# Windowed attention with a two-layer MLP: cross-partition copies and low parts on GpSimd, normalising on ScalarE

## The chip, the cores and the metric

The kernel runs on one core of one Trainium2 chip. A core has TensorE (PE in the profile), VectorE (DVE), ScalarE (ACT), GpSimd (POOL) and SyncE (SP), which issues the DMAs. The metric is the device time of one execution in microseconds, lower is better; several runs give a median.

## What is computed

```python
# attention: 8 batches, 8 heads, 576 tokens, head size 64, float32
scores = q @ k.T / sqrt(64)
mask_plain = (rel >= 0) & (rel < 32)                       # heads 0 to 3
mask_dil   = (rel >= 0) & (rel < 128) & (rel % 4 == 0)     # heads 4 to 7
attn = softmax(where(mask, scores, -1e9)) @ v
# MLP: x is the attention's result as [4608, 512]
h = x @ w_in                                               # [512, 2048]
g = h * clip(h + 3, 0, 6) / 6
out = g @ w_out                                            # [2048, 512]
```

rel is the query's position less the key's.

## The kernel before

**Precision.** Float32 matmuls are done as three matmuls of a cheaper kind: each factor is split into a high part (a rounded copy) and a low part (what the copy left out), and high x high, high x low and low x high are added up in PSUM.

**Attention** is cut into 48 trios (a group of four heads and a third of a batch's rows, 12 query blocks of 32 rows each). The first 12 are done in an opening whose order is written out by hand. The other 36 are done in blocks on TensorE (`attend`): a block multiplies the scores of trio b and the values of trio b-2. For the scores DVE adds the mask (L264) and takes the row maxima (L290), POOL scales the maxima (L294), ACT takes the exponents (L302, six groups of 64 columns), DVE transposes 32 by 32 blocks (`turn_by_blocks`, L404 and L405), and ACT copies the parts that must change partitions (`cross`, L412, four copies of 32x192, tile `a`).

For the values the result must be divided by its row sums. There are two ways. A trio in `SHARED` (17 of the 36) has DVE make the reciprocals (`share`, L310, L311) and ACT multiply, six operations of 64 columns (`shares`, L321). The other 19 are normalised by DVE alone (`normalise`, L326, L327, L329). Either frees the PSUM bank. Then the result `x` goes the same way as the exponents: DVE transposes, and ACT copies across partitions (L412, tile `xf`). What follows (`high`, L477, and `low`, L483 and L485) splits it for the MLP or copies it into `raw`; `low` is on POOL here.

**The MLP** has two forms. The first 1536 tokens (four chunks of 384) are done plainly: `gemm1` (L571 to L573) into `ps_h`, ACT's `relu` (L579), DVE's `gate` (L582), the high part `gh` (L586, by ACT in the opening, by POOL afterwards), DVE's low part `gl` (L590), and `gemm2` (L621 to L623) two steps later. The other 3072 tokens, in three groups of 1024, use a scheme of seven products in place of eight: sums and differences of weight blocks are made once, split into high and low, written to DRAM (`sums` for the first layer, `rights` for the second) and streamed back through `ring` buffers. For each of 2 x 8 pairs of weight blocks `combine` has DVE add up the parts (L691) and make four sums (L699), ACT take the high part (L703, 128x1024), and DVE the low part (L708, 128x1024); then five DMAs of SP store them (`combo_out`, `combo_plain`). A group runs the first layer's products (L798 to L800), with copies and gates on ACT and DVE (L1111, L1118, L1071, L1076), and then the second layer's (L789), whose factors are split by ACT (L1252, `gh`) and DVE (L1256, `gl`).

**Order.** Behind the opening every operation is put into a plan with its engine, an estimated duration, what it waits for and which buffers it takes and frees. TensorE's order is given; `_in_time` works out a latest start for each operation and goes through the plan, taking on each engine what can start soonest, and among these the one that is due first. This fixes the order of ACT, DVE, SP and POOL, each of which works through its own in order.

Of the kernel before, what the change touches and what calls it, by code (L numbers as in the profile page):

```python
# [20 lines left out]
QB = 32  # L21
# [17 lines left out]
EVER = 1.0e6  # L39
# [5 lines left out]
LATER = 2  # L45
LANDING = 2.6
PE_MASKS = frozenset()
SHARED = frozenset((0, 1, 2, 3, 4, 7, 8, 9, 10, 11, 12, 13, 14, 15, 27, 28, 32))
POOL_LOWS = frozenset((10, 11))
BESIDE = {(0, 0): 1, (0, 1): 2, (0, 2): 1, (0, 3): 2, (0, 4): 1, (0, 5): 2, (0, 6): 1, (0, 7): 1, **{(1, k): 1 for k in range(7)}}  # L50
HIGH_BY = ("aaaaaaaa",) * 7
# [34 lines left out]
def windowed_attention_ffn(ctx: ExitStack, tc: tile.TileContext, qk, vp, w, mask, out, out_t):  # L86
# [23 lines left out]
    nc = tc.nc  # L110
# [11 lines left out]
    CH = TB * QB  # L122
# [94 lines left out]
    es, ats, xs, xfs = {}, {}, {}, {}  # L217
# [187 lines left out]
        nc.vector.transpose(out=dst.rearrange("p (u i y) -> p u i y", u=2, y=QB), in_=twice)  # L405
        return dst, mid

    def cross(dst, mid, i):

        for c in (2 * i, 2 * i + 1):  # L410
            u, to = c % 2, c ^ 1
            ins = nc.scalar.copy(  # L412
                dst[QB * to : QB * (to + 1), u * CH // 2 : (u + 1) * CH // 2], mid[QB * c : QB * (c + 1), : CH // 2]
            )
        return ins


# [288 lines left out]
    def combo_low(side, k, i, n, eng):  # L706
        v, hi = (x[:, i * 4 // n : (i + 1) * 4 // n] for x in combos[side, k])
        eng.tensor_tensor(out=v.bitcast(F32R), in0=v, in1=hi.bitcast(F32), op=ALU.subtract)  # L708
# [10 lines left out]
    def combo_out(side, k):  # L719
        v, hi = combos.pop((side, k))  # L720
        for part, x in enumerate((hi.bitcast(F32), v)):
            if side:
                to = rights.rearrange("(i k) p a x -> k p i a x", k=PAIRS)[k][:, 0:4, part]
            else:
                to = sums[row(k, S2) : row(k, S2) + 4].rearrange("n p a x -> p n a x")[:, :, part]
            nc.sync.dma_start(out=to, in_=x)
# [111 lines left out]
    def op(engine, us, do, after=(), lag=0.0, takes=(), gives=(), before=(), ahead=AHEAD):  # L838
        plan.append(Operation(engine, us, do, [x for x in after if x is not None], lag, [(*x, 0)[:3] for x in takes], list(gives), list(before), ahead))
        if engine == "PE":  # L840
            beats.append(len(plan) - 1)
        return len(plan) - 1

    def transfer(us, size, do, after=(), takes=(), gives=(), ahead=EVER):
        x = op("SP", us, do, after, takes=takes, ahead=ahead)
        return op("DMA", size * 1.3, lambda: None, [x], lag=LANDING, gives=gives, ahead=EVER)

    ONE, TWO, SLOT = [("work", 1)], [("work", 2)], [("w", 1)]
# [1 line left out]
    raw_seen, freed = set(), []  # L850
    released = {"ps_h": [], "ps_a": freed}

    def turn_over(t, src, into, name, after):
        two = []

        def do():
            two.extend(turn_by_blocks(src.pop(t), name))
            into[t] = two[0]

        x = op("DVE", 0.92, do, [after], takes=TWO, gives=ONE, ahead=EVER)  # L860
        return [
            op("ACT", 0.7, lambda i=i: cross(*two, i), [x], gives=ONE if i else (), ahead=EVER) for i in range(2)
        ]

    def attend(bs, pools, whole=False):

        scores = [NFIRST + b for b in bs if NFIRST + b < T]
        values = [NFIRST + b - 2 for b in bs if b >= 2]
        couples = [(NFIRST + b, NFIRST + b - 2) for b in bs]
        order = [t for x in couples for t in x if t in scores + values]  # L870
        bank, room = dict(zip(order, pools)), {}

        def do():
            for x in couples:
                block(*(t if t in bank else None for t in x), [bank.get(t) for t in x], whole)

        names = {x: "ps_h" if bank[x] is ps_h else "ps_a" for x in order}
        for x in names.values():
            room[x] = room.get(x, 0) + 1
        beat = op(  # L880
            "PE", 0.35 + 0.3 * sum(by_tensor(t) for t in scores) + 0.535 * len(order), do,
            [*(x for t in values for x in turned[t]), *(landed_k.get(t) for t in scores), *(landed_v.get(t) for t in values),
             *(freed.pop(0) for _ in range(room.get("ps_a", 0)) if freed), *released["ps_h"][-2:][: room.get("ps_h", 0)]],
            takes=list(room.items()), gives=[("work", len(values))],
        )
        for ts in scores:
            x = beat
            if not by_tensor(ts):
                x = op("DVE", 0.55, lambda ts=ts: add_mask(ts), [beat], takes=ONE, gives=[(names[ts], 1)], ahead=EVER)
                released[names[ts]].append(x)  # L890
            x = op("DVE", 0.55, lambda ts=ts: plain_largest(ts), [x], ahead=EVER)
            x = op("POOL", 0.3, lambda ts=ts: scaled(ts), [x], ahead=EVER)
            for i in range(3):
                holds = not i and by_tensor(ts)
                x = op(
                    "ACT", 0.54, lambda ts=ts, i=i: exponents(ts, i), [x], takes=ONE if holds else (),
                    gives=[(names[ts], 1)] if i == 2 and by_tensor(ts) else (), ahead=EVER,
                )
            if by_tensor(ts):
                released[names[ts]].append(x)  # L900
            turned[ts] = turn_over(ts, es, ats, "a", x)
            if ts + NLOAD < T:
                landed_k[ts + NLOAD] = transfer(0.4, 0.82, lambda ts=ts: load_qk(ts + NLOAD), [beat])
        for tv in values:
            if tv - NFIRST in SHARED:
                x = op("DVE", 0.35, lambda tv=tv: share(tv), [beat], ahead=EVER)
                for i in range(3):
                    x = op(
                        "ACT", 0.5, lambda tv=tv, i=i: shares(tv, i), [x], takes=() if i else ONE,
                        gives=[(names[tv], 1)] if i == 2 else (), ahead=EVER,  # L910
                    )
            else:
                x = op("DVE", 0.9, lambda tv=tv: normalise(tv), [beat], takes=ONE, gives=[(names[tv], 1)], ahead=EVER)
            released[names[tv]].append(x)
            x = turn_over(tv, xs, xfs, "xf", x)
            if tv + NLOAD < T:
                landed_v[tv + NLOAD] = transfer(0.4, 0.77, lambda tv=tv: load_v(tv + NLOAD), [beat])
            pieces = [(n, place_of(token)[0]) for _, n, _, _, token in spans(tv)]
            kind = trios[tv][1]
            if any(c >= PLAIN for n, c in pieces):  # L920
                x = [*x, ends_of[1], *(combined[1, k][0] for k in range(PAIRS) if combo_place(1, k) == 1)]
            touched = {c for n, c in pieces if c >= PLAIN and (c, kind) not in raw_seen}
            raw_seen.update((c, kind) for c in touched)
            places = {}
            for c in touched:
                place = ("x1", 1) if (c - PLAIN, kind) in IN_ROOM else ("w", 1, 1)
                places[place[0]] = (place[0], places.get(place[0], (0, 0))[1] + 1, *place[2:])
            plain = [n for n, c in pieces if c < PLAIN]
            if plain:
                x = [op("ACT", sum(0.15 + n / 500 for n in plain), lambda tv=tv: high(tv), x, ahead=EVER)]  # L930
            split[tv] = op(
                "POOL", sum(0.25 + n / 250 for n, _ in pieces), lambda tv=tv: low(tv, nc.gpsimd), x, takes=list(places.values()), gives=ONE, ahead=EVER
            )
# [25 lines left out]
    def combine(side, k):  # L959
        place = combo_place(side, k)  # L960
        slots = "w" if place == "w" else f"x{place}"
        x = op(
            "DVE", 0.69, lambda: combo_words(side, k, 0, nc.vector), takes=[(slots, 2, SPARE[side][k])] if place == "w" else [(slots, 1, 1)],
            ahead=LEAD_SUMS,
        )
        words[side, k] = x = op("DVE", 0.69, lambda: combo_words(side, k, 1, nc.vector), [x], ahead=EVER)
        for i in range(4):
            x = op("DVE", 0.42, lambda i=i: combo_sum(side, k, i, nc.vector), [x], ahead=EVER)
        x = op("ACT", 1.05, lambda: combo_high(side, k), [x], takes=() if place == "w" else [(slots, 1)], ahead=EVER)
        x = op("DVE", 1.25, lambda: combo_low(side, k, 0, 1, nc.vector), [x], ahead=EVER)  # L970
        combined[side, k] = [
            transfer(0.9, 2.0, lambda: combo_out(side, k), [x], gives=[(slots, 2)]),
            transfer(1.35, 1.5, lambda: combo_plain(side, k), [x]),
        ]

    def last_use(side, f, x):
# [353 lines left out]
    with tc.manual_schedule(  # L1330
# [3 lines left out]
        for name in ORDER.split():  # L1334
            name, _, behind = name.partition("@")
# [261 lines left out]
```

## Time and profile before

| | |
|---|---|
| time, median of 3 runs | 830.58 us (830.51 to 830.89) |
| the profiled execution | 830.1 us, span 828.3 us, clock 0.995 |
| PE busy | 812.6 us (98%) |
| DVE busy | 634.7 us (77%) |
| ACT busy | 563.4 us (68%) |
| POOL busy | 128.5 us (16%) |
| ACT, copies of `xf` and of `a` (L412) | 50.4 and 50.4 us, 144 each of 350 ns |
| DVE, low parts of the sums (L708) | 20.7 us, 16 of 1294 ns |

The span is the time from the first to the last instruction of the profiled execution; busy time is the union of an engine's instructions. A line such as L412 is a line of the kernel. In a row of a group, the count is followed by the busy time in us, the mean of one in ns, the idle time of the engine just before these instructions, and what ended that idle time. In a row of the order of time stand the start, the duration (of several merged instructions together) and the instruction, with the idle time before it in brackets.

### The profile page before, as it was taken

What the parts mean: (1) busy time and instruction counts of PE and PEld (TensorE: products, weight loads), DVE (VectorE), ACT (ScalarE), POOL (GpSimd) and SP (SyncE); (2) the same over time, 40 slices, a digit from 0 to 9 for tenths busy, and PEclk for the clock granted to TensorE, in tenths of its full rate; (3) what the DMA queues carried; (4) which work ended last, traced back from release to release, by engine and by line L of the source; (5) the groups of instructions that cost most, each with busy time, mean ns of one, the idle gap of its engine ahead of it and who ended that gap; (6) DMA issues with size and microseconds to landing.
All of it is one profiled execution on the core that took longest, in us unless ns stands there. A gap on an engine that the chain in (4) does not pass through costs nothing.

```text
span 828.3 us, 20418 instructions
## 1 busy us (share of the span) xinstructions
PE 812.6 (98%) x8076; PEld 684.5 (83%) x8076; DVE 634.7 (77%) x1131; ACT 563.4 (68%) x1277; POOL 128.5 (16%) x192
## 2 busy tenths in 40 slices
PE   7999999999999999999999999999999999999998
PEld 4788999888889889888778888888888888888886
DVE  4989996568889898989869996665798834459943
ACT  3788776357997896879998564787656525446542
POOL 1338432112231224100121000010000000000000
PEclk9999999999999999999999999999999999999999
DMA  8757433257964989899885736867539379454632
GB/s 290 254 205 229 128 103 108 95 170 243 350 215 147 299 299 348 264 366 394 322 263 185 270 147 208 285 224 247 211 121 349 109 235 340 161 174 158 218 138 77
DMA packets 99455, 185.23 MB, mean 224 GB/s; under 512 B 6560, under 2 KB 35232, under 8 KB 99360
## 3 DMA queue, kind: packets, MB, share of 16 engines
q1 hardware_dynamic: 99360, 183.93, 64.9%
q8 instruction: 64, 1.05, 0.5%
q14 instruction: 31, 0.25, 0.1%
HBM read 145.10 MB, written 38.80 MB: 222 GB/s over the span
## 4 chain that ended last, share of the span: by engine, by line
PE 91%; ACT 5%; DMA 1%; DVE 1%; issue 1%; SPq 0%; DVEq 0%; ACTq 0%
PE ps_o L789 27%; PE ps_x L798 8%; PE ps_x L799 8%; PE ps_x L800 8%; PE ps_o L622 5%; PE ps_o L623 5%; PE ps_o L621 5%; PE ps_h L571 5%; PE ps_h L573 5%; PE ps_h L572 5%; PE ps_a L256 2%; PE ps_a L238 2%; DMA first<-in_v 1%; PE ps_b L256 1%; PE ps_b L238 1%
## 5 line engine op out<-in xcount | busy, mean ns | idle before, releaser
L789 PE MATMUL ps_o<-gh,ring 128*128 128x512 f32 x672 | 209.5, 389 | 0.7 <-ACT gh L1252 0.7
L789 PEld LDWEIGHTS ps_o<-gh,ring 128*128 128x128 f32 x672 | 126.1, 188 | 27.7 <-ACT gh L1252 1.5
L798 PE MATMUL ps_x<-cell,ring 128*128 128x512 f32 x336 | 132.5, 394 | 0.0
L789 PE MATMUL ps_o<-gl,ring 128*128 128x512 f32 x336 | 130.9, 390 | 0.6 <-DVE gl L1256 0.6
L799 PE MATMUL ps_x<-cell,ring 128*128 128x512 f32 x336 | 131.0, 390 | 0.0
L800 PE MATMUL ps_x<-cell,ring 128*128 128x512 f32 x336 | 130.8, 389 | 0.0
L1252 ACT CAST gh<-g 128x512 fp32r<-128x512 f32 x168 | 98.5, 620 | 46.1 <-PE ps_o L789 43.4
L1256 DVE TENSOR_TENSOR gl<-g,gh 128x512 fp32r<-128x512 f32 x168 | 109.5, 686 | 19.9 <-ACT gh L1252 9.1
L571 PE MATMUL ps_h<-x,wi 128*128 128x384 f32 x256 | 88.0, 344 | 0.2 <-DVE t L582 0.2
L573 PE MATMUL ps_h<-x,wi 128*128 128x384 f32 x256 | 86.2, 337 | 0.0
L572 PE MATMUL ps_h<-x,wi 128*128 128x384 f32 x256 | 85.9, 335 | 0.0
L623 PE MATMUL ps_o<-wo,gl 128*128 128x512 f32 x192 | 75.8, 395 | 0.0
L622 PE MATMUL ps_o<-wo,gh 128*128 128x512 f32 x192 | 75.6, 394 | 0.0
L621 PE MATMUL ps_o<-wo,gh 128*128 128x512 f32 x192 | 74.8, 389 | 0.3 <-PE ps_a L374 0.3
L789 PEld LDWEIGHTS ps_o<-gl,ring 128*128 128x128 f32 x336 | 63.1, 188 | 14.1 <-DVE gl L1256 1.2
L798 PEld LDWEIGHTS ps_x<-cell,ring 128*128 128x128 f32 x336 | 63.1, 188 | 13.8
L800 PEld LDWEIGHTS ps_x<-cell,ring 128*128 128x128 f32 x336 | 63.1, 188 | 13.3
L799 PEld LDWEIGHTS ps_x<-cell,ring 128*128 128x128 f32 x336 | 63.1, 188 | 12.9 <-DVE cell L773 0.4
L520 POOL TENSOR_SCALAR va<-st 128x512 f32<-128x512 f32 x32 | 53.9, 1688 | 75.0 <-DMA st<-in_w 67.0
L579 ACT ACTIVATE t<-ps_h,three 128x384 f32<-128x384 f32 x64 | 37.2, 583 | 40.4 <-PE ps_h L573 36.6
L302 ACT ACTIVATE e<-e,mx 128x64 f32<-128x64 f32 x216 | 56.6, 345 | 4.7 <-POOL mx L294 4.5
L1221 DVE TENSOR_TENSOR g<-g 128x1024 f32<-128x1024 f32 x48 | 57.4, 1217 | 0.0
(103 smaller groups left out, 1503.8 us busy)
## 6 DMA issues: line engine op xcount, KB each, us to landing
ring<-sums SPq DMA_DIRECT2D x84, 512.0 KB, 7.6
ring<-rights SPq DMA_DIRECT2D x84, 512.0 KB, 6.5
st<-in_w SPq DMA_DIRECT2D x32, 512.0 KB, 4.0
kq<-in_qk SPq DMA_DIRECT2D x39, 416.0 KB, 4.7
v<-in_v SPq DMA_DIRECT2D x39, 390.0 KB, 5.4
sums<-wi SPq DMA_DIRECT2D x24, 256.0 KB, 5.2
rights<-wo SPq DMA_DIRECT2D x24, 256.0 KB, 7.7
out<-o SPq DMA_DIRECT2D x11, 512.0 KB, 3.4
```

What stands on the lines that cost most here:

```text
L571: nc.tensor.matmul(ph, lhsT=wt(f, 0)[:, ks], rhs=a, start=(kt == 0), stop=False)
L572: nc.tensor.matmul(ph, lhsT=wt(f, 0)[:, ks], rhs=b, start=False, stop=False)
L573: ins = nc.tensor.matmul(ph, lhsT=wt(f, 1)[:, ks], rhs=a, start=False, stop=(kt == NK - 1))
L621: nc.tensor.matmul(po[c][tt], lhsT=gh[:, rows], rhs=wt(f, 2), start=first, stop=False)
L622: nc.tensor.matmul(po[c][tt], lhsT=gh[:, rows], rhs=wt(f, 3), start=False, stop=False)
L623: return nc.tensor.matmul(po[c][tt], lhsT=gl[:, rows], rhs=wt(f, 2), start=False, stop=(f == NF - 1))
L789: nc.tensor.matmul(banks[part], lhsT=right[:, a, cols], rhs=x, start=(start and not i), stop=(i == 2), skip_group_check=True)
L798: nc.tensor.matmul(bank, lhsT=tile_[:, 0, ks], rhs=h[:, kt], start=(start and kt == 0), stop=False, skip_group_check=True)
L799: nc.tensor.matmul(bank, lhsT=tile_[:, 0, ks], rhs=l[:, kt], start=False, stop=False, skip_group_check=True)
L800: nc.tensor.matmul(bank, lhsT=tile_[:, 1, ks], rhs=h[:, kt], start=False, stop=(kt == 1), skip_group_check=True)
L1252: nc.scalar.copy(two[0], gated_tile(g, q, k))
L1256: nc.vector.tensor_tensor(out=two[1], in0=gated_tile(g, q, k), in1=two[0].bitcast(F32), op=ALU.subtract)
```

## The change

Three things change. The four copies of each result across partitions (`xf`) go from ACT to POOL; those of the exponents (`a`) stay on ACT. All 36 later results are normalised by `share` and `shares`, that is by ACT with DVE's reciprocals; before it was 17. And the low part of the block sums is made by POOL in two halves of 128x512, where DVE made it in one operation; the stores wait for both halves. The durations given to the planner for these operations change with them.

```diff
-SHARED = frozenset((0, 1, 2, 3, 4, 7, 8, 9, 10, 11, 12, 13, 14, 15, 27, 28, 32))
+SHARED = frozenset(range(36))
...
-    def cross(dst, mid, i):
+    def cross(dst, mid, i, copy):
         for c in (2 * i, 2 * i + 1):
             u, to = c % 2, c ^ 1
-            ins = nc.scalar.copy(
-                dst[QB * to : QB * (to + 1), u * CH // 2 : (u + 1) * CH // 2], mid[QB * c : QB * (c + 1), : CH // 2]
-            )
+            ins = copy(dst[QB * to : QB * (to + 1), u * CH // 2 : (u + 1) * CH // 2], mid[QB * c : QB * (c + 1), : CH // 2])
         return ins
...
-    def turn_over(t, src, into, name, after):
+    def turn_over(t, src, into, name, after, by_pool=False):
...
         return [
-            op("ACT", 0.7, lambda i=i: cross(*two, i), [x], gives=ONE if i else (), ahead=EVER) for i in range(2)
+            op(
+                *(("POOL", 1.0) if by_pool else ("ACT", 0.7)),
+                lambda i=i: cross(*two, i, nc.gpsimd.tensor_copy if by_pool else nc.scalar.copy),
+                [x], gives=ONE if i else (), ahead=EVER,
+            )
+            for i in range(2)
         ]
...
-            x = turn_over(tv, xs, xfs, "xf", x)
+            x = turn_over(tv, xs, xfs, "xf", x, True)
...
-        x = op("DVE", 1.25, lambda: combo_low(side, k, 0, 1, nc.vector), [x], ahead=EVER)
+        lows_ = [op("POOL", 1.45, lambda i=i: combo_low(side, k, i, 2, nc.gpsimd), [x], ahead=EVER) for i in range(2)]
         combined[side, k] = [
-            transfer(0.9, 2.0, lambda: combo_out(side, k), [x], gives=[(slots, 2)]),
-            transfer(1.35, 1.5, lambda: combo_plain(side, k), [x]),
+            transfer(0.9, 2.0, lambda: combo_out(side, k), lows_, gives=[(slots, 2)]),
+            transfer(1.35, 1.5, lambda: combo_plain(side, k), lows_),
         ]
```

## The prediction

> **What bounds the kernel now.** I read the page first (busy time, waits), then the stages by window, then the order of single instructions where TensorE lost time.
>
> ```profile
> span 828.3 us, 20418 instructions
> PE 812.6 (98%) x8076; PEld 684.5 (83%) x8076; DVE 634.7 (77%) x1131; ACT 563.4 (68%) x1277; POOL 128.5 (16%) x192
> ```
>
> ```profile
> 160.00:336.00 176.00, 175.13 (x2585) 156.25 (x2585) 147.05 (x318) 140.68 (x420) 48.12 (x94) 1.00 0.77 253
> 336.00:371.00 35.00, 35.00 (x519) 28.22 (x518) 32.17 (x64) 27.19 (x62) 4.02 (x5) 1.00 0.91 307
> 371.00:433.00 62.00, 60.37 (x901) 48.14 (x899) 49.02 (x106) 59.56 (x152) 10.26 (x32) 1.00 0.92 327
> ```
>
> The window rows give the stretch, its length, then busy time of PE, PEld, DVE, ACT, POOL, the clock, DMA. TensorE is busy 98% and the clock is full (1.00). So the ceiling of any gain is what PE still loses, and the change touches only 160 to 583 us: before it runs the opening, written out by hand, after it no attention is left. Inside that, one stretch stands out: in 371 to 433 us ACT is busy 59.56 of 62.00 us (96%) and PE loses 1.6 us by the busy count. There ACT sets the pace. The rows give start, duration, and in brackets the idle time and what ended it:
>
> ```profile
> 429.20 0.39 PE L799 MATMUL ps_x<-cell,ring 128*128 128x512 f32 x1
> 429.42 0.39 PE L800 MATMUL ps_x<-cell,ring 128*128 128x512 f32 x1
> 430.14 0.50 PE L789 MATMUL ps_o<-gh,ring 128*128 128x512 f32 x1 [0.33 <-ACT gh L1252]
> 430.94 0.50 PE L789 MATMUL ps_o<-gl,ring 128*128 128x512 f32 x1 [0.30 <-DVE gl L1256]
> ...
> 431.97 0.40 PE L789 MATMUL ps_o<-gh,ring 128*128 128x512 f32 x1
> 432.72 0.50 PE L789 MATMUL ps_o<-gh,ring 128*128 128x512 f32 x1 [0.35 <-ACT gh L1252]
> 433.52 0.50 PE L789 MATMUL ps_o<-gl,ring 128*128 128x512 f32 x1 [0.29 <-DVE gl L1256]
> ```
>
> ACT in the same stretch, start and duration first:
>
> ```profile
> 428.00 1.44 ACT L412 COPY xf<-xf_t 32x192 f32<-32x192 f32 x4
> 429.46 0.62 ACT L1252 CAST gh<-g 128x512 fp32r<-128x512 f32 x1
> 429.99 0.58 ACT L1111 COPY s<-ps_x 128x512 f32<-128x512 f32 x1
> 430.59 1.44 ACT L412 COPY xf<-xf_t 32x192 f32<-32x192 f32 x4
> 432.05 1.14 ACT L1252 CAST gh<-g 128x512 fp32r<-128x512 f32 x2
> ```
>
> Matmul starts go every 0.22 us (429.20, 429.42). The four late ones start 0.72, 0.80, 0.75 and 0.80 us after the one before: 3.07 - 4 x 0.22 = 2.2 us lost. On ACT, four copies of a result across partitions (1.44 us) stand right ahead of each `gh` for which PE waits. These are the copies that the change takes off ACT.
>
> A second loss lies at 278 us, where the values of a block wait for copies of `a` (which stay on ACT):
>
> ```profile
> 277.65 0.24 PE L238 MATMUL ps_b<-kq 64*32 64x64 f32 x2
> 278.33 0.24 PE L256 MATMUL ps_a<-v,a 64*32 64x65 f32 x1 [0.38 <-ACT a L412]
> 279.06 0.24 PE L256 MATMUL ps_a<-v,a 64*32 64x65 f32 x1 [0.43 <-ACT a L412]
> ```
>
> 0.68 us passes between the first two starts, where such matmuls otherwise follow in hundredths; with the second wait of the same kind that is some 1.3 us.
>
> **The change part by part.**
>
> ```profile
> L412 ACT COPY xf<-xf_t 32x192 f32<-32x192 f32 x144 | 50.4, 350 | 2.3
> L321 ACT ACTIVATE x<-ps_a,z 128x64 f32<-128x64 f32 x84 | 19.3, 317 | 0.2
> L329 DVE TENSOR_TENSOR x<-ps_a,z 128x384 f32<-128x384 f32 x19 | 10.6, 558 | 0.9
> L708 DVE TENSOR_TENSOR v<-v,sh 128x1024 fp32r<-128x1024 f32 x16 | 20.7, 1294 | 0.4 <-ACT sh L703 0.2
> L485 POOL COPY raw<-xf 128x64 f32<-128x64 f32 x7 | 2.1, 300 | 9.3 <-ACT xf L412 8.4 <-DVE mx L290 1.0
> L485 POOL COPY raw<-xf 128x192 f32<-128x192 f32 x5 | 2.7, 531 | 16.1 <-DVE z L327 10.1 <-ACT xf L412 6.0
> L483 POOL TENSOR_TENSOR x<-xf,x 128x384 fp32r<-128x384 f32 x4 | 4.5, 1121 | 15.7 <-ACT x L477 15.7
> L483 POOL TENSOR_TENSOR x<-xf,x 128x192 fp32r<-128x192 f32 x3 | 2.1, 714 | 2.9 <-ACT x L477 2.9
> L520 POOL TENSOR_SCALAR va<-st 128x512 f32<-128x512 f32 x32 | 53.9, 1688 | 75.0 <-DMA st<-in_w 67.0 <-ACT wi L549 4.4 <-DVE va L539 1.4
> ```
>
> *Copies of the results.* 36 results x 4 copies leave ACT: 144 x 0.350 = 50.4 us. They go to POOL at a price the trace does not hold. Bounds: 0.300 us (64 columns) and 0.531 us (192 columns cut into strided pieces, on 128 partitions); a plain run of 192 lies between, I take 0.45. POOL +65 us, 1.8 us for a result instead of 1.4. What follows a copy is the copy into `raw` (L485), already on POOL and ahead of its need by far, so the longer latency costs nothing.
>
> *Normalising.* 19 results more go from DVE to ACT: DVE -19 x 0.558 = -10.6 us; the two small DVE operations on z stay; ACT +19 x 6 x 0.317 = +36.1 us. ACT in sum: -50.4 + 36.1 = -14.3 us, but by stage this differs. In 160 to 336 us four of the 19 (numbers 5, 6, 16, 17) add 4 x 1.90 = 7.6 us, and the copies of some 17 results go (17 x 1.40 = 23.8 us). In 336 to 371 four (18 to 21) add 7.6 us to 27.19 of 35 us, and no copies go there. In 371 to 433 five (22 to 26) add 9.5 us and these copies go:
>
> ```profile
> L412 ACT COPY xf<-xf_t 32x192 f32<-32x192 f32 x44 | 15.4, 350 | 0.7
> ```
>
> 59.56 - 15.4 + 9.5 = 53.7 us of 62. Over both stretches ACT ends at 88.4 of 97 us, two more than before, but the load moves to where ACT still had 7.8 us free. ACT then has 8 us of air in the stretch that ends in the 2.2 us loss, so I take all of that as gone.
>
> *Low parts of block sums.* 16 operations leave DVE (-20.7 us); 32 halves of 128x512 come to POOL. From 714 ns at 192 and 1121 ns at 384 columns the slope is 2.12 ns a column, 1.39 us at 512; bounds 1.12 and 1.69 us (a one-input POOL operation of that size). POOL +44 us, 2.8 us a sum instead of 1.29. Its five DMAs now wait for both halves, some 1.5 us later, and SP works in order, so ring loads and loads of keys and values queue behind. SP waits there already, longer than that:
>
> ```profile
> SPq L726 <- DVE v L708: 22.2, 9, 6.3
> ```
>
> Nine waits of the stores for L708, up to 6.3 us, reached no matmul by the waits of PE. So nothing for this; with that cover gone it would be the 1.5 us once or twice. POOL in sum: 128.5 + 65 + 44 = 238 us, 29% of the span; inside 160 to 433 us from 62 to some 155 of 273 us. Behind its new work queue the scaled maxima of the softmax (a block ahead of their use) and the 36 gates:
>
> ```profile
> 317.65 0.56 DVE L590 TENSOR_TENSOR gl<-t,gh 128x384 fp32r<-128x384 f32 x1 [0.60 <-POOL gh L586]
> 321.47 0.39 PE L621 MATMUL ps_o<-wo,gh 128*128 128x512 f32 x1
> ```
>
> This gate is the tightest of the 36: `gl` ends at 318.21 and PE takes it at 321.47, 3.3 us later. One half (1.39) or two copies (0.9) or both fit into that. Two halves and two copies, 3.7 us, do not: 0.4 us, which I count once.
>
> *Waits at 278 us.* ACT loses copies of results in 160 to 336 us and DVE 1.3 us for each sum, which gives the chain softmax, transpose, copies of `a` air; but the whole order behind the opening is planned anew from estimated durations. I take half of 1.3 us.
>
> **Sum.** -2.2 - 0.65 + 0.4 = -2.45 us. The profiled execution took 830.1 us, 1.8 us around its span of 828.3; the median of the runs is 830.58. So 827.65 for such an execution, 828.1 us as a median. About 0.2% (1.7 us) is what a measurement of this kernel tells from no change; the forecast is 0.3%.
>
> **The rivals.**
>
> *Nothing is gained.* The planner fills the freed ACT time with other work that stands ahead of `gh` in the same way (results 22 to 26 put six operations each there), and the wait at 278 us hangs on DVE's order. PE is at its pace elsewhere, so the time stays: 830.3 us.
>
> *POOL holds up the gates (the other side).* POOL works in order: a copy waiting for its DVE transpose, or a half waiting for the high part from ACT, holds every gate behind it. For it: the 16 sums run from 165.0 to 380.6 us and the gates (row below) from 163.7 to 337.0, so that 13 sums lie among them. Against: 3.3 us of cover at least. It decides where a hold exceeds 3.3 us. With halves at the 1.69 us bound, two halves and two copies make 4.4 us, 1.1 us a time; at a third of the 13 sums +4.8, less the 2.2: 833.2 us.
>
> *Banks held by ACT (the other side too).* A result normalised by DVE left its PSUM bank within some 0.9 us; by ACT it waits in a queue that is 90% full:
>
> ```profile
> 410.71 0.15 DVE L310 TENSOR_SCALAR z<-ps_b 128x6 f32<-128x6 f32 x1
> 415.13 0.52 ACT L321 ACTIVATE x<-ps_b,z 128x64 f32<-128x64 f32 x2
> ```
>
> Here from 410.71 to 415.65, 4.9 us, and no matmul waited, since the next block comes 42 matmuls of 0.22 us, 9.2 us, later. It decides when ACT falls more than 5 us further behind in 336 to 371 us (34.8 of 35 us by my count): 1 us at each of five blocks, +5 - 2.2: 833.4 us.
>
> *DVE and POOL block one another.*
>
> ```profile
> L590 DVE TENSOR_TENSOR gl<-t,gh x64: 517/553/1059, 42.0 to 338.4; 128x384 fp32r<-128x384 f32 x64
> L708 DVE TENSOR_TENSOR v<-v,sh x16: 1181/1218/1526, 165.0 to 380.6; 128x1024 fp32r<-128x1024 f32 x16
> L485 POOL COPY raw<-xf x73: 237/407/2928, 234.0 to 579.4; 128x96 f32<-128x96 f32 x16, 128x384 f32<-128x384 f32 x12, 128x128 f32<-128x128 f32 x11, 128x160 f32<-128x160 f32 x7
> L586 POOL CAST gh<-t x36: 498/567/1552, 163.7 to 337.0; 128x384 fp32r<-128x384 f32 x36
> ```
>
> Same shapes (minimum/median/maximum ns) take up to twice or thrice their median, on both engines, which looks like waiting for each other. A gate's chain could thus gain 0.5 (L590) + 1.0 (L586) behind one half and two copies (2.3): 3.8 us, 0.5 beyond the cover. At six such gates +3 us: 831.1. The Trainium skill, page "SBUF — State Buffer", section "SBUF: two separate sides", says that a DVE operation with two SBUF inputs and a GpSimd operation take the shared pair of ports by an exclusive lock, one blocking the other for a whole instruction. The spread of L590 and L586 agrees. By that rule alone all new POOL time under such DVE operations would come back as DVE time, and the 31 us taken off DVE would be no relief; the sum above does not use that relief save at 278 us.
>
> *More is gained.* All of 2.2 and 1.3 us and a little at other small waits before 433 us: 826.5 us.
>
> **How the numbers follow.** Forecast 0.44 (own range 826.8 to 828.9), nothing gained 0.20, POOL 0.12, banks 0.08, blocking 0.08, more 0.08. Faster by over 0.2%: nearly all of 0.44, the 0.08, a little of the second: 0.51. Slower: 0.20 and part of the blocking: 0.24. Same: 0.25. The range runs from a little under the case of more gain to 833.0, in the midst of the slow cases: 825.8 to 833.0.
>
> **What would show it.** Right: four POOL copies a result near 0.45 us; halves near 1.4 us; no result copies ahead of the first `gh` of the right halves and PE at 0.22 us there; ACT about 14 us less busy, DVE about 31. Wrong: a row of PE or PEld waiting for POOL `gh` or DVE `gl` L590 in 160 to 340 us (POOL), for ACT `x` L321 in 340 to 410 (banks), L590 and L699 with means far above 0.60 and 0.44 us (blocking), or the same loss at the turn to the right halves with other ACT work ahead of `gh` (nothing gained).

## The result, and the profile after

The changed kernel takes 840.74 us (median of 4 runs, 838.22 to 841.93) beside 830.74 us (830.51 to 831.10): ratio 1.0116, interval 1.0091 to 1.0141. It is slower by 10 us where 2.45 less were forecast. The profiled execution took 841.93 us, its span is 840.1. Most lines of the changed kernel have a number lower by two: L588 is L590 of before, L697 is L699, L706 is L708; behind the attention it is higher by three (L1255 for L1252).

The page, and the stages that were shown of before:

```profile
span 840.1 us, 20563 instructions
PE 815.9 (97%) x8076; PEld 687.4 (82%) x8076; DVE 626.1 (75%) x1096; ACT 536.0 (64%) x1247; POOL 230.4 (27%) x368
...
160.00:336.00 176.00, 172.70 (x2570) 153.81 (x2569) 144.18 (x304) 116.99 (x362) 106.14 (x185) 1.00 0.73 240
336.00:371.00 35.00, 29.53 (x399) 23.77 (x398) 30.03 (x47) 25.67 (x64) 21.05 (x24) 0.90 0.89 290
371.00:433.00 62.00, 59.60 (x900) 48.34 (x899) 40.92 (x92) 52.87 (x156) 20.55 (x59) 1.00 0.89 319
```

The loads moved the way that was meant: ACT has 27 us less, POOL 102 more. But in 336 to 371 us, where PE had been busy all 35, it is busy 29.53, and the clock is 0.90. To find where time went, I set the same matmul of both traces side by side, by its place in PE's order, and read how far it is behind (the lag). The lag grows by 1.8 us in the opening, which the change does not touch; in the traces of the other runs this part lies between 1.6 us less and 2.4 more. Then it grows by 1.4 at 220 to 250 us of the time before, falls by 1.6 at 280, grows by 3.1 at 295 to 311, by 7.5 at 336 to 340, by 2.1 at 375 to 400, and falls by 2.4 at 430 to 434. At the end it is 11.8 us.

The largest step, in PE's order of time (start, duration, idle before it):

```profile
340.87 0.39 PE L796 MATMUL ps_x<-cell,ring 128*128 128x512 f32 x1
346.73 0.80 PE L797 MATMUL ps_x<-cell,ring 128*128 128x512 f32 x1 [5.47 <-DVE cell L771]
347.32 0.63 PE L798 MATMUL ps_x<-cell,ring 128*128 128x512 f32 x1
347.75 0.63 PE L796 MATMUL ps_x<-cell,ring 128*128 128x512 f32 x1
...
348.61 0.63 PE L798 MATMUL ps_x<-cell,ring 128*128 128x512 f32 x1
```

PE starts the first seven-product group and waits 5.5 us for the low part of the tokens (L771). Then it goes at 0.43 us a matmul in place of 0.22, for eight of them: 1.7 us more. The cause is seen on POOL, then on DVE:

```profile
326.21 0.84 POOL L584 CAST gh<-t 128x384 fp32r<-128x384 f32 x1
327.04 0.23 POOL L294 TENSOR_SCALAR mx<-mx 128x6 f32<-128x6 f32 x1
327.23 2.08 POOL L483 COPY raw<-xf 128x32 f32<-128x32 f32 x4
329.21 2.73 POOL L706 TENSOR_TENSOR v<-v,sh 128x512 fp32r<-128x512 f32 x2
331.90 0.69 POOL L584 CAST gh<-t 128x384 fp32r<-128x384 f32 x1
332.54 2.82 POOL L483 COPY raw<-xf 128x128 f32<-128x128 f32 x6
335.21 0.64 POOL L584 CAST gh<-t 128x384 fp32r<-128x384 f32 x1
335.83 0.66 POOL L294 TENSOR_SCALAR mx<-mx 128x6 f32<-128x6 f32 x1
336.46 5.99 POOL L706 TENSOR_TENSOR v<-v,sh 128x512 fp32r<-128x512 f32 x3
```

```profile
336.31 1.21 DVE L764 TENSOR_TENSOR t<-raw,t 128x1024 f32<-128x1024 f32 x1
337.45 1.64 DVE L588 TENSOR_TENSOR gl<-t,gh 128x384 fp32r<-128x384 f32 x1
339.01 2.31 DVE L764 TENSOR_TENSOR t<-raw,t 128x1024 f32<-128x1024 f32 x1
...
345.46 1.21 DVE L771 TENSOR_TENSOR cell<-raw,cell 128x1024 fp32r<-128x1024 f32 x1
```

POOL works without a pause from 321 to 345 us. The last copies into `raw` that the first group needs end at 335.4 us. Before, this was the last of them, at 319.3:

```profile
318.40 0.94 POOL L485 COPY raw<-xf 128x96 f32<-128x96 f32 x3 [0.78 <-ACT xf L412]
```

So the tokens' differences (L764, before L766) start 16 us later (336.3 for 320.0), and beside halves of L706 they and `gl` also take longer: 2.31 us where 1.21 is usual, 1.64 where 0.55 is. The low part (L771) stands behind them on DVE. The 3.1 us at 295 to 311 come mainly from two waits of about 1 us each for DVE's gate (`t`, L580); what makes the gate late there was not followed further. The groups of the changed kernel and its two longest waits of PE for attention or tokens:

```profile
L588 DVE TENSOR_TENSOR gl<-t,gh 128x384 fp32r<-128x384 f32 x64 | 48.7, 761 | 13.6 <-POOL gh L584 7.0 <-ACT gh L584 3.6 <-PE ps_o L620 2.6
L697 DVE TENSOR_TENSOR v<-v 128x256 f32<-128x256 f32 x64 | 33.3, 538 | 0.3
L706 POOL TENSOR_TENSOR v<-v,sh 128x512 fp32r<-128x512 f32 x32 | 46.7, 1472 | 3.9 <-ACT sh L701 3.8
L412 POOL COPY xf<-xf_t 32x192 f32<-32x192 f32 x144 | 59.7, 414 | 90.0 <-DVE xf L405 55.5 <-ACT t L577 9.0 <-ACT ps_x L1133 9.0
...
PE ps_x L797 <- DVE cell L771: 5.5, 1, 5.5
PE ps_a L256 <- DVE e L264: 1.9, 1, 1.9
```

31.3 us of work were taken off DVE, and its busy time fell by 8.6 only: 22.7 us came back as longer operations. `gl` went from 602 to 761 ns, the block sums from 439 to 538. The second wait in the list is put down to DVE's `e`, but PE waited there for a load of values as well; see the rivals below.

At the turn to the right halves the forecast gain is there. PE no longer waits between the layers:

```profile
443.68 0.39 PE L798 MATMUL ps_x<-cell,ring 128*128 128x512 f32 x1
443.90 0.39 PE L787 MATMUL ps_o<-gh,ring 128*128 128x512 f32 x1
444.13 0.39 PE L787 MATMUL ps_o<-gl,ring 128*128 128x512 f32 x1
```

### The profile page after: what moved, and what is told of

It reads as the page before. It is cut to its first block, busy times and chain, and to the rows that moved or that the text cites. A ratio compares the mean times of both kernels' runs of the same rounds, so it can differ in the third digit from the quotient of the medians.

```text
span 840.1 us, 20563 instructions
## 1 busy us (share of the span) xinstructions
PE 815.9 (97%) x8076; PEld 687.4 (82%) x8076; DVE 626.1 (75%) x1096; ACT 536.0 (64%) x1247; POOL 230.4 (27%) x368
## 4 chain that ended last, share of the span: by engine, by line
PE 82%; DVE 6%; ACT 4%; POOL 3%; DMA 2%; issue 2%; SPq 0%; POOLq 0%; DVEq 0%; ACTq 0%
PE ps_o L787 27%; PE ps_x L796 9%; PE ps_x L797 9%; PE ps_x L798 9%; PE ps_o L620 4%; PE ps_o L619 4%; PE ps_o L621 4%; PE ps_h L569 4%; PE ps_h L571 3%; PE ps_h L570 3%; ACT a L412 1%; PE ps_a L238 1%; PE ps_b L256 1%; POOL xf L412 1%; DVE gl L588 1%
## 5 line engine op out<-in xcount | busy, mean ns | idle before, releaser
L1255 ACT CAST gh<-g 128x512 fp32r<-128x512 f32 x168 | 99.1, 620 | 49.8 <-PE ps_o L787 45.4
L412 POOL COPY xf<-xf_t 32x192 f32<-32x192 f32 x144 | 59.7, 414 | 90.0 <-DVE xf L405 55.5
L302 ACT ACTIVATE e<-e,mx 128x64 f32<-128x64 f32 x216 | 58.4, 348 | 5.7 <-POOL mx L294 5.7
```

The lines of the kernel that those rows point to most:

```text
L1255: nc.scalar.copy(two[0], gated_tile(g, q, k))
```

## The experiments

Theories: A, the halves of the low parts on POOL cause the loss, by POOL's time (A2) or because POOL and DVE block one another (A1); B, the copies of the results; C, any new order; D, ACT's multiplications. Ratios are to the kernel before on the same chip, with 95% intervals. The kernel before took 830.2 to 830.4 us there, single runs from 827.3 to 833.6.

**One part undone.** Edits against the changed kernel:

```diff
# lows_by_dve
-lows_ = [op("POOL", 1.45, lambda i=i: combo_low(side, k, i, 2, nc.gpsimd), [x], ahead=EVER) for i in range(2)]
+lows_ = [op("DVE", 1.25, lambda: combo_low(side, k, 0, 1, nc.vector), [x], ahead=EVER)]
# copies_by_act
-            x = turn_over(tv, xs, xfs, "xf", x, True)
+            x = turn_over(tv, xs, xfs, "xf", x)
# old_shares
-SHARED = frozenset(range(36))
+SHARED = frozenset((0, 1, 2, 3, 4, 7, 8, 9, 10, 11, 12, 13, 14, 15, 27, 28, 32))
```

> The changed kernel with one part undone: the low parts of the block sums are made by DVE in one operation again. In the trace of the changed kernel PE waits 5.5 us at 341 us for a low part of the tokens (L771), because the copies into raw end on POOL at 335.2 us instead of 318.9. Theory A (the halves of the sums are what fills POOL there, 46.7 us in all, and what stretches DVE's operations with two inputs in SBUF: L697 538 ns against 439, L588 761 against 602): the wait and the slow clock behind it go, PE has the 2.2 us at the turn to the right halves as a gain, 828 to 831 us, L588 near 0.60 us. Theory B (the copies of the results on POOL make raw late by themselves): the wait stays by more than half, 835 us or more. Theory C (any new order of the plan costs this much): 834 to 840 us.

Measured: 829.55 us, 0.9987 (0.9973 to 1.0002); a second time, with the following expectation, 829.78 us, 0.9993 (0.9975 to 1.0011).

> The changed kernel with the low parts of the block sums by DVE again, measured a second time with more rounds, to tell 0.2%: the two gains that the prediction named, 2.2 us at the turn to the right halves and 1.3 us at 278 us, should be seen in it, less small waits elsewhere: 828 to 830 us beside 830.4.

The whole loss is gone, as A says. PE has no wait for the tokens left, `gl` takes 601 ns. The gain at the turn is in both traces (the lag falls by 2.4 us in each), but the time is not told from that of before: new small waits take part of it back, 1.3 us in each at 232 to 252.

> The changed kernel with the copies of the results across partitions back on ACT; the halves stay on POOL and all 36 results are normalised by ACT. ACT is then at 536 + 50 = 586 us. Theory A: POOL still has the halves, so raw is late still, if less, since 60 us of copies are gone from its queue: 833 to 838 us. Theory B: raw is in time, the loss at 341 us goes: 829 to 832 us, unless ACT, which is then over 95% busy in 336 to 433 us, loses it there. Theory C: 834 to 840 us.

Measured: 852.92 us, 1.0275 (1.0260 to 1.0290), far worse than each theory said. PE waits 4.9 us until 440 us and 3.2 until 280 for the copies of `a` on ACT; in 420 to 440 us ACT is busy 19.35 of 20. With all results normalised by ACT, the copies cannot stay there.

> The changed kernel with the former set of 17 results normalised by ACT, the other 19 by DVE; copies of the results and halves on POOL. Theories A and B both: POOL's load is the same, so raw is late and the wait near 341 us stays: 836 to 841 us. A rival D (banks or results late through ACT's multiplications cause the loss): 829 to 833 us.

Measured: 841.49 us, 1.0129 (1.0102 to 1.0156): as A and B, and D falls. The wait for the tokens is 4.9 us.

**One part alone**, on the kernel before:

> The kernel before with one part of the change alone: the low parts of the block sums are made by POOL in two halves. Theory A: most of the loss is here without the other two parts: 835 to 840 us, POOL's halves near 1.47 us, L588 or its like well above 0.60 us. Theory B: POOL has room enough for 47 us more (175 us busy), 829 to 832 us. Theory C: 834 to 840 us, but with other waits than for the tokens' low parts.

Measured: 843.41 us, 1.0161 (1.0143 to 1.0179). POOL is less full here, and yet the loss is larger than A foresaw. DVE and POOL where PE's first long wait comes from:

```profile
273.94 3.47 DVE L697 TENSOR_TENSOR v<-v 128x256 f32<-128x256 f32 x3
277.33 0.36 DVE L404 STREAM_TRANSPOSE a_t<-e 128x192 f32<-128x192 f32 x1
...
273.90 2.69 POOL L706 TENSOR_TENSOR v<-v,sh 128x512 fp32r<-128x512 f32 x2 [0.42 <-ACT sh L701]
```

Three block sums, 1.3 us by their mean before, take 3.47 beside two halves of 2.69, so the transpose behind them is 2 us late, then the copies of `a` on ACT, and PE waits 3.2 us. The larger step, 7.8 us of lag, comes at 336 to 340 us of the time before:

```profile
342.40 1.05 ACT L701 CAST sh<-v 128x1024 fp32r<-128x1024 f32 x1 [3.70 <-DVE v L697]
343.53 2.80 POOL L706 TENSOR_TENSOR v<-v,sh 128x512 fp32r<-128x512 f32 x2 [0.79 <-ACT sh L701]
345.13 2.59 DVE L697 TENSOR_TENSOR v<-v 128x256 f32<-128x256 f32 x3
346.35 0.57 PE L796 MATMUL ps_x<-cell,ring 128*128 128x512 f32 x1 [3.33 <-ACT cell L767]
348.90 0.80 PE L797 MATMUL ps_x<-cell,ring 128*128 128x512 f32 x1 [1.99 <-DVE cell L771]
```

Here the copies into `raw` had ended at 325.6 us, in time. But ACT waits 3.7 us for block sums that DVE makes beside halves, with the high part of the tokens (L767) behind them, and DVE's low part stands behind three more such sums (2.59 us).

> The kernel before with one part of the change alone: the copies of the results across partitions go to POOL (60 us). Theory A: POOL has room, since no halves are there, and the four copies ahead of the first high part of the right halves at 430 us are gone: 826.5 to 829.5 us, 1 to 3 us faster. Theory B: raw is late by itself: 833 us or more.

Measured: 830.72 us, 1.0002 (0.9987 to 1.0017): no loss, so B falls, and no gain. The lag in its trace falls by 2.4 us at the turn and 1.5 at 280, and grows by 3.1 at 374 to 400 us, where PE waits for values still in transfer (3.4 us in three waits).

> The kernel before with one part of the change alone: all 36 results are normalised by ACT, the copies stay there too. ACT has then 87 + 17 = 104 us of work in the 97 us from 336 to 433 us: the load is too much there, PE waits 5 to 9 us: 835 to 840 us. If ACT's work can be put off past 433 us, 830 to 832.

Measured: 844.33 us, 1.0164 (1.0144 to 1.0184), worse than expected. ACT is then the bound at the turn:

```profile
PE ps_o L787 <- ACT gh L1255: 5.0, 1, 5.0
```

With the kernel before and the changed one, all eight combinations of the three parts are now measured. Without the halves, the copies on POOL cost nothing, alone or with the shares (830.72, 829.55), and the shares without them cost 14 us (844.33). With the halves every combination is slower than before: 843.41 alone, 841.49 with the copies, 852.92 with the shares, 840.74 with both.

**What in the halves costs it.** The changed kernel with other work in place of the halves, the same plan and waits:

```diff
# halves_unread
-        eng.tensor_tensor(out=v.bitcast(F32R), in0=v, in1=hi.bitcast(F32), op=ALU.subtract)
+        for _ in range(3):
+            eng.memset(v, 0.0)
# halves_tiny
+        eng.memset(v[:, 0, :1], 0.0)
```

> The changed kernel, where each half of the low parts on POOL is replaced by three memsets of the same 128x512 (the low parts are zero: what the high part leaves out of the block sums is lost). Plan, order and waits are the same, and POOL is busy for about as long, but it reads nothing from SBUF there. Theory A1 (the halves hurt because a POOL operation that reads SBUF and a DVE operation with two SBUF inputs keep each other waiting): DVE's L588 and the block sums (L697, L689) go back to near 0.60, 0.44 and 0.70 us, and most of the loss goes: 828 to 833 us. Theory A2 (the halves hurt because they fill POOL's queue and raw stands behind them): DVE's operations are short again, but the wait at 341 us stays: 836 to 841 us, provided the memsets of a half take 1.2 us or more together; if they are much shorter, this run cannot tell.

Measured: 839.36 us, 1.0103 (1.0084 to 1.0123). POOL's time is there (three times 527 ns, 1.58 us a half where the real ones take 1.47), DVE's operations are nearly as short as before, and PE still waits:

```profile
L588 DVE TENSOR_TENSOR gl<-t,gh 128x384 fp32r<-128x384 f32 x64 | 39.9, 623 | 18.7 <-POOL gh L584 13.1 <-PE ps_o L620 3.5 <-ACT gh L584 1.9
L697 DVE TENSOR_TENSOR v<-v 128x256 f32<-128x256 f32 x64 | 27.6, 448 | 0.3
L707 POOL MEMSET v<- 128x512 f32 x96 | 50.0, 527 | 7.7 <-ACT sh L701 3.9
...
PE ps_x L798 <- DVE cell L772: 3.1, 1, 3.1
```

> The changed kernel, where each half of the low parts on POOL is replaced by one memset of a single column (what the high part leaves out of the block sums is not made). Plan, order and waits stay those of the changed kernel; only POOL's time goes. Theory A2 (POOL's time: the queue that holds gates, copies of results and raw is full from 315 to 345 us): raw ends 10 us or more earlier, PE's wait for the tokens' low parts goes, 828 to 832 us. Theory C (the new order costs this, whoever does the low parts): 836 to 840 us as with the memsets of full length (839.4).

Measured: 830.46 us, 1.0002 (0.9990 to 1.0013). The new order costs nothing in sum: the loss comes with what POOL does in the halves. Where POOL was busy 28.30 of 30 us in the changed kernel, here (fifth figure behind the length):

```profile
315.00:345.00 30.00, 29.99 (x235) 26.27 (x235) 27.56 (x49) 19.85 (x47) 15.50 (x33) 1.00 1.05 373
...
326.15 3.01 POOL L483 COPY raw<-xf 128x128 f32<-128x128 f32 x6
...
PE ps_a L256 <- DMA v<-in_v: 1.8, 1, 1.8
```

`raw` ends at 329.2 us, 10 us later than before, and nothing waits for it; at 334.7 (unread) and 335.4 (changed) PE waits 3.1 and 5.5 us. The lag of this trace shows what belongs to the order alone: it grows by 1.5 us at 220 to 250, by 1.0 at 295 to 313 and by 1.9 at 375, and falls by 1.6 at 280 and by 2.4 at the turn. So the forecast gains are made, and waits of the new order take them back. With POOL's time in the halves, the growth is 3.1 at 295 to 311 and 7.5 at 336 to 340.

The same two edits on the kernel with the halves alone:

> The low parts on POOL as the only part of the change, each half replaced by three memsets of 128x512, 1.58 us together, that read nothing (the low parts of the sums are zero). With the real halves this kernel took 843.4 us. At 274 us three block sums on DVE took 3.47 us together, beside a half, in place of 1.2, and the copies of a for which PE waits came behind them. If blocking between POOL and DVE is the cause here: 829 to 834 us, block sums near 0.44 us. If POOL's time or the order is the cause: 839 to 844 us.

> The low parts on POOL as the only part, each half replaced by a memset of one column (the low parts are not made). Blocking or POOL's time as the cause: 829 to 832 us. The order as the cause, with ACT as full as before the change and its copies of results in other places: 836 to 843 us.

Measured: 833.63 us, 1.0035 (1.0019 to 1.0051), and 834.11 us, 1.0044 (1.0030 to 1.0058). Here it is the other way: POOL's time without its reads costs nothing beside the tiny one, and of the 13 us of the real halves 10 go when they read nothing, which is blocking; 3 to 4 are the order. The step at 336 to 340 us is gone from both traces; at 278 PE still waits 1.8 us. Block sums and `gl` of the unread one:

```profile
L588 DVE TENSOR_TENSOR gl<-t,gh 128x384 fp32r<-128x384 f32 x64 | 38.2, 598 | 15.1 <-POOL gh L584 8.0 <-PE ps_o L620 3.5 <-ACT gh L584 3.5
L697 DVE TENSOR_TENSOR v<-v 128x256 f32<-128x256 f32 x64 | 27.4, 454 | 0.3
```

**Half of the halves**, for one layer's sums only, the other layer's by DVE:

> The changed kernel with POOL's halves only for the eight sums of the first layer's weights, those of the second layer by DVE. In the trace before, the first eight low parts end at 280 us, the last eight run from 291 to 381 us, beside the copies into raw that PE's products at 341 us hang on. Theory A2: without the second eight the queue is free when it matters: most of the loss goes, 829 to 834 us. If the place does not matter, half of the loss: 834 to 836 us.

> The changed kernel with POOL's halves only for the eight sums of the second layer's weights, those of the first layer by DVE. Theory A2: these stand in POOL's queue with the copies into raw: most of the loss is here, 835 to 841 us. If the place does not matter: 834 to 836 us.

> The changed kernel with POOL's halves for the second layer's sums only, a second time with more rounds; it took 828.55 us, ratio 0.998. If that is real: 827.5 to 829.5 us and an interval below 1. If it was chance: 829.5 to 831.

Measured: first layer 833.88 us, 1.0033 (1.0015 to 1.0052); second layer 828.55 us, 0.9980 (0.9963 to 0.9996), and again 830.70 us, 0.9993 (0.9975 to 1.0010). My reading that the second layer's halves are the harmful ones was wrong: alone they cost nothing. The losses of the two do not add up to the 10 us. In both, `raw` ends early enough (325 to 327 us); only together do they make it late. In the first layer's trace two other waits of PE stand out: 2.5 us for a load of values, and 1.5 for a low part of the tokens though `raw` was there. The gain of the first run was not found again, so no version here is shown to beat the kernel before.

**The planner's durations.**

> Low parts of the sums by DVE, copies of results by POOL, all results normalised by ACT, and the planner given the durations that the traces show for six operations (two exponents 0.70 for 0.54, two shares 0.64 for 0.50, two copies on POOL 0.83 for 1.0, the high part on POOL 0.67 for 0.55, a block sum 0.46 for 0.42, a low part 0.62 for 0.58). If small waits come from an order made for shorter operations: 827 to 829 us; if the order does not matter so much: 829 to 831; a new order may also hit new waits, 832 or more.

Measured: 837.21 us, 1.0071 (1.0059 to 1.0083). Truer durations made a worse order; the lag grows at several places (3.9 us at 309 to 320, 1.9 at 375, 2.4 at 435 to 466 us). I did not follow up why.

## Why the prediction was wrong

**The step that failed** is the account of POOL's queue, +0.4 us in the sum. For what stands behind the new work it counted the scaled maxima and the 36 gates, and set the copies into `raw` aside: "What follows a copy is the copy into `raw` (L485), already on POOL and ahead of its need by far, so the longer latency costs nothing." I had read no row for that cover. Alone, the four copies bear the sentence out (830.72 us); with the halves in the same queue it fails. The cover is some 10 us: at 329.2 us `raw` is still in time, at 335.4 PE waits 5.5 us and then runs at half speed, 7.5 us of lag in all. I put the new POOL work into a mean (155 of 273 us; it came to 148), while it falls together: in 315 to 345 us POOL is busy 28.30 us. A queue that is half empty over a stage can be full for 30 us of it. And I priced each new operation for what waits for it, where what counts is what stands behind it on POOL.

**Blocking was put too low.** I saw it in the rows; in the sum it is nothing, and as a rival 3 us from six gates with a chance of 0.08. 22.7 of the 31.3 us taken off DVE came back. The port rule that the prediction cited from the Trainium skill, page "SBUF — State Buffer", section "SBUF: two separate sides", agrees with the runs: with halves that read nothing DVE's block sums have nearly their old length (448 ns, before 439, with the real halves 538). But by how much it sets the time depends on what else is late. With the halves alone it is some 10 us (843.4 against 833.6), most of it at 336 to 340 us, where DVE's sums stood ahead of the parts of the tokens. In the changed kernel it is 1.4 us that the intervals do not tell apart (840.7 against 839.4). The memsets are a little longer there than the real halves, and these are themselves lengthened by blocking (1.26 us at the least, 1.47 in the mean), so how the 10 us divide between POOL's time and blocking is not measured exactly.

**Rows misread.** The row of L321 has 84 operations in 19.3 us, 0.23 us each, because they overlap; the prediction took their mean duration of 0.317 and so +36.1 us where the row gives +26. ACT therefore lost 27 us of load and not 14. The row of L329 with 19 operations is not that of the 19 results: after the change 12 of it are left, from the opening, and 12 of the 19 stood in a row of `ps_b`. The mean is 558 ns in both, so the 10.6 us are right by luck. And the spread of L485 mixes shapes, which says nothing on blocking. None of these made the loss.

**The rivals.** "POOL holds up the gates" named the engine and the side, but not the place: the late matmul waits for tokens, not for `gh`. "Banks held by ACT" as the cause of this loss falls with old_shares. The growth at 375 us begins at a load of values on SP that lands at 388.42, after PE needed it (about 386.7); it was issued at 381.88, behind the stores of a sum. I had put such a delay at nothing. It belongs to the new order and not to POOL's time, since PE waits 1.8 us for such a load in halves_tiny too.

**What was right, and how far.** The loss at the turn to the right halves goes: the four late matmuls win back 2.2 us of 2.2. That it went because the copies of results left ACT is not shown. These rows are of the changed kernel and of lows_alone, both right ahead of the turn:

```profile
442.27 1.44 ACT L412 COPY a<-a_t 32x192 f32<-32x192 f32 x4
...
442.38 1.44 ACT L412 COPY xf<-xf_t 32x192 f32<-32x192 f32 x4
```

In the changed kernel four copies of `a` of the same length stand there, and in lows_alone and its two stand-ins the copies of results are still on ACT; yet PE goes on at 0.22 us in all of them, and the lag falls by 2.4 us. In both traces ACT has made a `gh` (L1255, from 441.1) ahead of the copies, so a new order on ACT, or PE coming later, can be enough, and the gain as forecast is in part luck. The loss at 278 us goes too in the changed kernel, 1.6 us where I took 0.65. Copies took 0.414 us (0.45), halves 1.47 (1.39), both within their bounds. Together 4.0 us were gained; 14.1 were lost in the profiled execution beside the 1.8 of the opening.

## What to carry to other kernels

Before work goes to an engine that looks idle, look at what already stands in its queue, and read for each such operation when it ends and when the bound engine needs it; a mean of 27% busy says nothing about the 30 us in which everything falls due. Whether a move costs occupancy or contention is told by two cheap stand-ins in the same order: one as long that reads nothing, one with no length. The parts of a change are to be tried alone and together, since their costs do not add: copies to POOL alone and second-layer halves with the rest cost nothing, shares alone cost 14 us and halves alone 13, all at once 10.

## What the runs showed of the hardware

A wait of PE can cost more than its length. After 5.5 us of waiting eight matmuls went at 0.43 us instead of 0.22, and the granted clock was half:

```profile
346.00:351.00 5.00, 4.27 (x10) 3.38 (x11) 4.60 (x6) 1.71 (x3) 1.37 (x1) 0.52 1.04 366
```

After a wait of 3.1 us (halves_unread) the first six matmuls started at full speed and the next eight took 0.43 us each. The Trainium skill, page "TensorE: Matmul & The Clock Gate", section "Part 1: The HAM clock gate", has the clock at half after an idle window of about 3.4 us; the wait of 5.5 us agrees with that, the one of 3.1 us is shorter, and the drop came some 1.5 us after the restart. Shorter waits went either way. The first row is of halves_unread after a wait of 1.9 us, the second of the changed kernel around one of the same length:

```profile
386.30:389.50 3.20, 3.20 (x32) 2.45 (x18) 1.51 (x6) 0.00 (x0) 0.23 (x1) 0.50 1.06 394
386.00:390.00 4.00, 2.13 (x150) 1.81 (x134) 2.31 (x5) 2.45 (x4) 3.13 (x7) 1.00 1.04 391
```

So the length of the wait alone does not decide it in these traces; what does, they do not show.

A GpSimd operation on 128x512 with two inputs can hold a DVE operation of two SBUF inputs for most of its own length: beside such halves (1.47 us in the mean) `gl` took 1.64 us for 0.55, and a difference of the tokens 2.31 for 1.21. It is held itself: three halves took 5.99 us where three means are 4.4. Memsets on GpSimd did not do this: beside them the block sums took 448 and 454 ns, before 439.
